# Loading the values of batch 0 once, in slots of three pools, under a newly written order of all steps

## The chip, the cores and the metric

One core of a Trainium2 chip runs the kernel as one program. The time is that of the device in microseconds (us), the median of several executions. The engines are TensorE (PE, with its weight loads as PEld), VectorE (DVE), ScalarE (ACT), GpSimd (POOL) and SyncE (SP), whose queue issues every transfer of this kernel.

## What is computed

A sparse attention and two feed-forward blocks follow one another (4 batches, 8 heads, 576 tokens, 64 numbers a head):

```python
scores = scale * np.matmul(q, k.transpose(0, 1, 3, 2))
thresh = np.max(scores, axis=-1, keepdims=True) - tau
scores = np.where(scores >= thresh, scores, -1000000000.0)
attn = softmax(scores)                                # exp, divided by its sum
x = np.matmul(attn, v)                                # 2304 tokens x 512
h = x @ w_in                                          # 2304 x 2048
g = P(h) / (Q(h) + 1e-06)                             # cubic over quadratic
x = g @ w_out                                         # 2304 x 512
y = ((x @ w1) * (x @ w2)) @ w3 @ w_out2               # 2304 x 512
```

## The kernel before

Every product that feeds the second decimal half of the result is made of two half-precision parts, a high one and a low one ("split"), so that most matmuls come in threes. The heads are taken in pairs: four pairs `c` for each batch `b`. A pair is worked through in two units: `u=0` takes the query blocks 0 and 1, `u=1` the blocks 2, 3 and the short block 4.

One block goes through these steps: `qk` (scores on PE, two PSUM tiles "S"), `top` (row maxima on DVE), `thr`, `exp` (on ACT, its second half on ACT or DVE), `recip`, `p_norm`, `p_hi` and `p_lo` (split of the probabilities), and `p_t` (a transposing DMA into a tile "pT"). When all blocks of a unit are there, `pv` multiplies by the values on PE and `x_split` takes the result from PSUM.

The values of a pair are raw `f32` numbers in DRAM. Their scale is found per batch: `square_v` (ACT) sums the squares of five of the nine row groups of each pair, and `scale_v` makes the power of two. `split_v` then makes the tiles "vh" and "vl" of a pair, in two instructions. In the kernel before, `load_v` brings the values twice: five row groups (320 KB) for `square_v`, and later all nine (576 KB) for `split_v`. Both go into one of the three slots of the pool "wr", which the raw weights (`raw_w`, 512 KB each) use as well. The pool "pT" has three slots too.

The weights are loaded raw, put together again by `conv_w` (two instructions), squared (`square_w`) and, for `w_in`, reduced over PE (`norm_w`) to a scale (`scale_w`). Only with that scale can `split_w` make the two parts of any piece of `w_in`, and only then can the first `h_product` start. `w_product` folds `w3` and the last weight into one matrix ahead of that. After it come `h_product`, the activations, `turn` (a transposing DMA) and `y_product` for each token tile of the first block, and `ab_product`, `turn` and `o_product` for the second.

The order of all these steps is written out by hand as a text, `ORDER`. A token such as `54v.0.1` is event 54, its engine ("v" or nothing DVE, "a" ACT, "p" POOL), and the slots of the tiles that it opens. An event with several parts stands there several times. Each engine, and SP's queue, runs its instructions in the order of the text, so that a transfer whose slot is not yet free holds back all transfers that stand behind it.

Of the kernel before, what the change touches and what calls it, by code (L numbers as in the profile page):

```python
# [16 lines left out]
AF = mybir.ActivationFunctionType  # L17
# [15 lines left out]
0 49.0 4.1 51p.0 5.0.0 51.0 15.0.1 1 16v 53.2 55v.1 55.1 6.1 7.1 26.0.1 29.0 28.0 30 22.2.3 32p.0  # L33
31p.0 31.2 34.0.4 36.5 36a 34a 13.2 24a 38a 38 40v 54.0.1 56.1 42a.6 44p 8.1 58 9.0 3 10.0 11.1
159.7.8 21.1 12 48p.0 12.0 50 46.0 18.0 60v.1 62.1.1 62a 52.1 12 14v.0.0 14 23a.1 17.2 20v.1.1
23.3 64.4 64a 94.0.1 66p 66 68a 20 19a.0 37.0 96.2 76p.5 98 78 90.0.6 100v.2 39p.1 25.1 70a.4 80
39.4 27p.1 72v 74 19.5 102.2.1 104.5 102v 41.2 27.6 57.1 104v 106p 123.1.0 106 117v.4 119 109a
125.3 111p.2 113v 92a 45.0 33.1 115.2 127 43a.0 43.7 63.2 82.0.0 47a.1 47.8 86.0 161v 129a.0 121.0
131.3.3 133.5 131a 57 65v.0 35p.1 35.9 133a 163.0.1 57 165.0 167 169v.1 84a 171.4.1 171a 65.10
173.2 135p 88v.2.2 135 77.1 173a 79p.1 145a.4 88 118.2 79.11 137a 191.0.1 84 81.0 67.1 147 149  # L40
193.1 195 120p.0 120.12 57 71.0 71 198p.2 200.5.0 59a.13 83v.1 139p.6 83.14 202.5 69p.0 200a 202a
228.0.1 204a 204 105.2 175a 175 185v.4 107a.1 177a 108.0 141p 143 214a.3 69.15 110a.0 71 122.1
230.2 187 216 232 110.16 189.1 234a.0 236.6.5 238.2 124v.0 124.17 238a 236a 85.1 85 71 73a.18
256.0.1 95.0 151.0 179p.6 181v 258.3 153a 107.19 645.1 153 260 647v.0 262a.1 218 91.2 112.0
224.4.7 264.7.8 266.1 266a 85 240v 264a 647.20 97p.1 174.1 240 93p.0 97.21 242a 93.22 206a 250v.3
226v 292 625.0 85 252 294.0.1 295.0 297 126.2 112 183.0 112 208p.2 87v.23 176a.1 112 254.2 299v.2
176.24 114v.25 617.1 301.0.6 302.3 116.0 268p 268 128v.0 270v 128.26 210p 628p.1 272v.0 628.27
651.1 212 301a 134.0 302a 654v.1 654.28 274p 278a.2 99.0 166.2 304p 304 168a.0 2 155.1 617 136p.1
617 244v.8 617 280 136.29 306v 246v 130.1 282 168.30 313v.1 157v.3.3 157 315 318.1.0 320.1 150.0
308p.7 620a.31 152v.1 99 152.32 322 323p.0 138.0 325.1.5 142.2 144a.0 288.2.3 144.33 656.1 656 656  # L50
99 309p 99 631.1 327.6 327v 634p.1 325v 634.34 329p 182.0 213.2 343.1 101a.35 329 637.0 215a.0 637
637 158.1 184p.1 637 656 184.36 215.37 221.0 190.2 330a 332v.4 160a.1 345.2 160.38 223v.0 659a.39
223.40 132.1 140 639v.41 146.1 623.0 154.0 220.0 148 290a 346v.1 197.1 199p.1 222a 334v 348.2.5
192v.0 192.42 229.0 199.43 205.2 156 222 156 231v.0 231.44 348v 245.1 170.1 162.0 164.0 172 207p.1
207.45 178.0 180 186.1 188 188 350a 371.0.1 89.0 373.3 194.0 196.1 201.1 203 209.0 247p.0 225.1
211 227.0 237.0 248.0 247.46 374 239v.1 233.0 350 352p 239.47 235 217.1 219 219 249.0 331.2 333p.0
# [1177 lines left out]
```

## Time and profile before

| what | value |
|---|---|
| time, median of 3 (lowest to highest) | 1035.44 us (1033.13 to 1037.77) |
| profiled execution: its time, its span | 1034.65 us, 1032.8 us |
| PE busy | 966.9 us, 94% of the span |
| DVE, ACT, POOL busy | 811.3, 662.0, 313.7 us |
| moved by DMA | 154.63 MB, mean 150 GB/s |

A share of the whole span is an average over stages with different limits. So the profile is read by stretch: which engine is busy without gaps there, and what PE, which is the busiest, waits for.

### The profile page before, as it was taken

The numbers are of one execution on the slowest core, as the hardware profiler recorded it, in microseconds if no ns is written. First come the engines' busy times: TensorE is split into PE (matmuls) and PEld (weight loads), VectorE is DVE, ScalarE is ACT, GpSimd is POOL, SyncE is SP. The second block draws the span as 40 slices with busy tenths as digits, with TensorE's granted clock in tenths as the row PEclk, the third lists the DMA queues.
The fourth block names the chain that finished last, engine by engine and source line by source line (L and its number), as shares of the span: only waits on it lengthen the run. The fifth ranks groups of instructions, "written<-read, shape, count | busy, mean of one in ns | idle before, by whom it ended". The sixth has DMA issues, their size and how long they took to land. (4 is left out here: it accounts for less than half of the span.)

```text
span 1032.8 us, 15597 instructions
## 1 busy us (share of the span) xinstructions
PE 966.9 (94%) x5280; PEld 462.6 (45%) x5284; DVE 811.3 (79%) x1595; ACT 662.0 (64%) x1227; POOL 313.7 (30%) x345
## 2 busy tenths in 40 slices
PE   2599887799999999999999999999999999999998
PEld 1244343344444445554444454544544445444443
DVE  4667789998777998889889989889878857676831
ACT  4464589987657798788647787787664434454510
POOL 2223233424322324233332432333423121223210
PEclk9999989899999999999999999999999999999999
DMA  7999797777757785899665768776666444444332
GB/s 240 243 251 260 250 238 207 185 201 175 189 113 151 157 174 103 172 197 178 126 134 104 143 131 177 153 149 134 129 123 119 93 90 88 80 65 71 62 72 61
DMA packets 334623, 154.63 MB, mean 150 GB/s; under 512 B 307408, under 2 KB 311504, under 8 KB 334544
## 3 DMA queue, kind: packets, MB, share of 16 engines
q1 hardware_dynamic: 334544, 153.65, 66.6%
q8 instruction: 41, 0.67, 0.3%
q14 instruction: 38, 0.31, 0.1%
HBM read 69.98 MB, written 8.13 MB: 76 GB/s over the span
## 5 line engine op out<-in xcount | busy, mean ns | idle before, releaser
L868 PE MATMUL y<-wp,gt 128*128 128x512 f16 x864 | 200.0, 379 | 0.9 <-DMA gt<-gg 0.8
L804 PE MATMUL h<-wp,xp 128*128 128x512 f16 x768 | 179.7, 382 | 3.5 <-DVE U L826 2.9
L975 PE MATMUL h<-wp,yy 128*128 128x512 f16 x576 | 132.2, 379 | 1.1 <-ACT r L819 0.5
L868 PEld LDWEIGHTS <-gt 128*128 128x128 f16 x864 | 82.8, 98 | 105.2 <-issue 6.5
L521 DVE TENSOR_REDUCE m<-S 128x1 f32<-128x576 f32 x144 | 104.7, 750 | 17.1 <-PE S L512 11.7
L804 PEld LDWEIGHTS <-xp 128*128 128x128 f16 x768 | 73.6, 99 | 99.0 <-issue 14.6
L512 PE MATMUL S<-raw 64*128 64x288 f32 x512 | 87.7, 449 | 20.4 <-ACT p L548 10.3
L1004 PE MATMUL y<-wp,gt 128*128 128x512 f16 x432 | 100.2, 379 | 0.0
L812 ACT ACTIVATE U<-h,cf 128x512 f32<-128x512 f32 x72 | 55.8, 775 | 62.9 <-PE h L804 42.0
L975 PEld LDWEIGHTS <-yy 128*128 128x128 f16 x624 | 60.1, 98 | 76.0 <-issue 6.0
L543 ACT ACTIVATE S<-S,th 128x576 f32<-128x576 f32 x107 | 74.7, 712 | 28.3 <-DVE th L359 15.9
L352 POOL TENSOR_TENSOR gg<-A,r 128x512 f16<-128x512 f32 x38 | 52.2, 1374 | 125.9 <-DVE A L847 74.7
L352 POOL TENSOR_TENSOR hl<-p,hl 128x576 f16<-128x576 f32 x48 | 64.6, 1348 | 70.6 <-DVE hl L340 32.3
L548 ACT ACTIVATE p<-S,xy 128x576 f32<-128x576 f32 x107 | 78.9, 742 | 2.9 <-DVE hl L352 0.5
L512 PEld LDWEIGHTS S<-raw 64*128 64x128 f32 x512 | 48.4, 195 | 60.7 <-ACT p L548 19.2
L834 ACT ACTIVATE r<-A,lnb 128x512 f32<-128x512 f32 x72 | 51.8, 721 | 34.8 <-DVE A L352 19.0
L843 DVE SCALAR_TENSOR_TENSOR gg<-U,cf,r 128x512 f16<-128x512 f32 x72 | 56.3, 783 | 20.9 <-ACT r L836 11.7
L352 POOL TENSOR_TENSOR A<-A,r 128x512 f32<-128x512 f32 x37 | 48.3, 1305 | 78.0 <-ACT r L819 75.0
L925 PE MATMUL h<-cw 128*128 128x512 f32 x128 | 60.8, 629 | 9.8 <-DVE cw L680 8.8
L680 DVE SCALAR_TENSOR_TENSOR cw<-rw,head 128x512 int32<-128x512 int32 x72 | 51.9, 725 | 18.3 <-POOL head L340 13.7
L1004 PEld LDWEIGHTS <-gt 128*128 128x128 f16 x432 | 41.7, 98 | 51.5 <-issue 2.2
L728 PE MATMUL y<-cw,dg 128*128 128x512 f32 x112 | 61.8, 634 | 3.0 <-ACT wp L336 1.6
(196 smaller groups left out, 1676.9 us busy)
## 6 DMA issues: line engine op xcount, KB each, us to landing
rw<-in_moe_w_dram SPq DMA_DIRECT2D x32, 511.8 KB, 4.5
rw<-in_moe_w_out_dram SPq DMA_DIRECT2D x24, 511.8 KB, 4.8
raw<-in_k_dram SPq DMA_DIRECT2D x32, 288.0 KB, 3.4
wr<-in_v_dram SPq DMA_DIRECT2D x16, 576.0 KB, 4.8
rw<-in_moe_w_in_dram SPq DMA_DIRECT2D x16, 511.8 KB, 4.3
wr<-in_v_dram SPq DMA_DIRECT2D x16, 320.0 KB, 3.4
out_dram<-A SPq DMA_DIRECT2D x16, 256.0 KB, 2.4
d_y<-x SPq DMA_DIRECT2D x13, 256.0 KB, 2.4
```

The costliest lines, as they stand in the source:

```text
L352: (nc.gpsimd if eng[0] == "p" else nc.vector).tensor_tensor(o, x, y, op=op)
L512: nc.tensor.matmul(t[s][:, half, :HS], x[r, o:o + 128], y[r, keys], start=True, stop=True)
L521: nc.vector.tensor_reduce(st["m", b, c, blk][:, s:s + 1], t[:, :, :HS], axis=AX.XY, op=ALU.max, negate=True)
L543: nc.scalar.activation(t, t, AF.Prelu, bias=th, alpha=BIG)
L548: nc.scalar.activation(x, t, AF.Exp, bias=xy[:, 0:1], accum_out=su)
L728: nc.tensor.matmul(y, st["dg", dg], r, start=True, stop=False)
L804: nc.tensor.matmul(t, x[:, y, c, o:o + 128], w[:, a, :], start=c + i == 0, stop=c == KD - 1 and i == 2)
L843: stt(p[:, 0, :], u, cf[:, 3:4], r, ALU.add, ALU.mult)
L868: nc.tensor.matmul(st["y", n], x[:, 4 * a + j, :], w[:, y, :], start=f + j + i == 0, stop=f == 3 and j == 3 and i == 2)
L925: nc.tensor.matmul(t, st["cw", ("w3", m, j // 4)][:, o:o + 128], st["cw", ("wo2", j)], start=j == 0, stop=j == 7)
L975: nc.tensor.matmul(t, x[:, 4 * y + c, :], w[:, a, :], start=c + i == 0, stop=c == KD - 1 and i == 2)
L1004: nc.tensor.matmul(st["o", n], x[:, 4 * a + j, :], w[:, y, :], start=hf + j + i == 0, stop=hf == 1 and j == 3 and i == 2)
```

## The change

For batch 0 the five-group load is gone. `load_v` with nine groups is called in its place, ahead of `square_v`, which reads the first five groups of that tile; the tile stays until `split_v`. Pair 0 keeps its place in the pool "wr", pairs 1, 2 and 3 go into the three slots of the pool "pT", which the transposed probabilities use afterwards. Batches 1 to 3 load as before. All steps stand in a new order, and many have another engine.

```diff
 ORDER = """
-0 49.0 4.1 51p.0 5.0.0 51.0 15.0.1 1 16v 53.2 55v.1 55.1 6.1 7.1 26.0.1 29.0 28.0 30 22.2.3 32p.0
...
-2527.1 2527 2533 2533 2449 2521 2534a.1 2534
...
     def load_v(b, c, n):
-        t = T("wr", [128, 9, 2 * D])[:, :n, :]
+        t = T("wr" if b or c == 0 else "pT", [128, 9, 2 * D])[:, :n, :]
...
-        nc.scalar.activation(j, st.pop(("vr", b, c, 5)), AF.Square,
+        nc.scalar.activation(j, st.pop(("vr", b, c, 5)) if b else st["vr", b, c, 9][:, 0:5], AF.Square,
...
-            at(load_v, b, c, 9)
+            if b:
+                at(load_v, b, c, 9)
             at(split_v, b, c)
...
     def norms_v(b):
         for c in range(NP):
-            at(load_v, b, c, 5)
+            at(load_v, b, c, 5 if b else 9)
```

The text of the order has 3958 tokens before and 3954 after. Written out, the places of some steps (counted in tokens) are these:

| step | before | after |
|---|---|---|
| first `load_v` of pairs 0, 1, 2, 3 of batch 0 | 2, 12, 35, 39 | 29, 28, 36, 19 |
| second `load_v` of the same pairs | 26, 48, 111, 282 | none |
| last part of `split_v` of the same pairs | 55, 66, 140, 297 | 57, 67, 50, 232 |
| `pv` of the first unit of the same pairs | 108, 203, 359, 428 | 127, 194, 346, 430 |
| last `raw_w` of `w_in` | 404 | 380 |
| first matmul of `split_w` of `w_in` | 442 | 451 |

And these are the engines that the letters name:

| step | before: DVE, ACT, POOL | after: DVE, ACT, POOL |
|---|---|---|
| `exp`, second half | 37, 107, 0 | 30, 114, 0 |
| `conv_w`, first half | 22, 18, 32 | 29, 19, 24 |
| `p_hi`, first head of a pair | 23, 26, 31 | 16, 28, 36 |
| `p_lo`, first head of a pair | 32, 0, 48 | 26, 0, 54 |
| `den` | 35, 0, 37 | 31, 0, 41 |
| `split_v`, first half | 8, 8, 0 | 5, 11, 0 |
| `scale_q` | 11, 16, 5 | 6, 16, 10 |

## Rows read from the trace of the kernel before

**Rows 1.** The page: busy time of the engines, share of the span, instructions.

```profile
PE 966.9 (94%) x5280; PEld 462.6 (45%) x5284; DVE 811.3 (79%) x1595; ACT 662.0 (64%) x1227; POOL 313.7 (30%) x345
```

**Rows 2.** Busy time by stretch; behind it granted clock, DMA share, GB/s.

```profile
0.00:47.00 47.00, 18.43 (x74) 9.35 (x76) 24.95 (x56) 22.80 (x47) 11.93 (x22) 1.00 0.84 239
47.00:120.00 73.00, 68.23 (x229) 31.24 (x226) 50.78 (x91) 34.14 (x65) 20.23 (x27) 0.95 0.92 257
120.00:135.00 15.00, 8.82 (x53) 4.62 (x50) 12.17 (x26) 12.96 (x26) 6.94 (x7) 0.82 0.91 259
135.00:208.00 73.00, 58.66 (x266) 25.52 (x262) 66.11 (x142) 67.42 (x140) 26.94 (x28) 0.90 0.80 206
208.00:316.00 108.00, 104.98 (x540) 49.15 (x542) 88.48 (x204) 75.36 (x142) 31.23 (x33) 1.00 0.70 170
316.00:988.00 672.00, 667.94 (x3952) 324.81 (x3951) 558.39 (x1059) 443.83 (x801) 211.78 (x224) 1.00 0.63 126
988.00:1033.00 45.00, 39.87 (x185) 17.92 (x183) 10.39 (x20) 5.44 (x9) 4.69 (x5) 0.97 0.29 65
```

**Rows 3.** Waits of PE up to 210 us: in total, times, longest.

```profile
PE S L512 <- ACT p L548: 9.6, 4, 4.9
PE h L925 <- DVE cw L680: 8.8, 3, 6.6
PE h L696 <- ACT sq L687: 3.7, 5, 2.0
```

**Rows 4.** Waits of SP's queue up to 135 us: in total, times, longest.

```profile
SPq L669 <- DVE cw L680: 27.4, 21, 4.0
SPq L584 <- DVE cw L680: 13.9, 4, 6.0
```

**Rows 5.** The timeline around the first split of the input weights.

```profile
118.64 5.32 SPq L669 DMA_DIRECT2D rw<-in_moe_w_in_dram  x3
...
125.31 4.50 ACT L687 ACTIVATE sq<-cw 128x512 bf16<-128x512 f32 x8
...
135.47 1.52 PE L728 MATMUL y<-cw,dg 128*128 128x512 f32 x2
```

**Rows 6.** DMA issues: count, KB each, median us from issue to landing.

```profile
wr<-in_v_dram SPq DMA_DIRECT2D x16, 576.0 KB, 4.8
...
rw<-in_moe_w_in_dram SPq DMA_DIRECT2D x16, 511.8 KB, 4.3
wr<-in_v_dram SPq DMA_DIRECT2D x16, 320.0 KB, 3.4
```

**Rows 7.** Groups by line, shapes kept apart: busy us, mean ns of one.

```profile
L352 POOL TENSOR_TENSOR hl<-p,hl 128x576 f16<-128x576 f32 x48 | 64.6, 1348 | 70.6 <-DVE hl L340 32.3 <-ACT hl L336 31.0 <-DVE sc L439 2.9
...
L546 DVE SCALAR_TENSOR_TENSOR p<-S,th,p 128x576 f32<-128x576 f32 x37 | 29.7, 812 | 8.6 <-ACT p L541 7.8 <-issue 0.9
...
L352 DVE TENSOR_TENSOR hl<-p,hl 128x576 f16<-128x576 f32 x32 | 24.8, 776 | 3.2 <-ACT hl L336 1.9 <-POOL hl L340 0.8
```

**Rows 8.** One DVE line with two inputs in SBUF: min/median/max ns.

```profile
L845 DVE SCALAR_TENSOR_TENSOR A<-A,gg x72: 672/691/1648, 162.1 to 979.2; 128x512 f32<-128x512 f32 x72
```

More of the change, by code (lines that the diff above doesn't have):

```diff
@@ new lines @@
+93.2 207 110 248 112a.25 652.1 621.1 211 256 258v.1 260.7.2 95a.1 136.1 650.26 95.27 262.3 652
+237v 124.0 260a 262a 126v.0 624p.1 264v 219.0.5 97 264 221a 266a 624.28 274v.8 276 97 99a.29
+290.1.0 126.30 291.0 87.0 163.2 293 165v.1 613.0 148.1 165.31 150v.0 652 140.0 150.32 213 627.2
+295p.2 297.0.4 298.3 298a 613 142p.1 142.33 240p.6 297a 314.0.1 316.1 318 319v.0 630p.0 73.0 210.1
+288 321.1.5 630.34 212v.1 212.35 613 321a 613 616a.36 619.0 250.0 218.0 300p 339.0 300 302v 242p
+341.2 278 179.2 181v.0 633.0 128.0 155.1 220p.1 304p.1 309p.7 220.37 311 157p.1 633 633 284.0.8
@@ new lines @@
+157.38 633 305v 635a.39 181.40 268a.3 652 655v.41 187.0 215.0 217v 217 189p.1 194.1 226.2 342a.1
+189.42 270v 130.1 234.0 196v.0 344.2.4 196.43 202.1 344v 236p.1 286a 365 138 159.0 658.1 161.0
+167.0 169 175.1 183.0 228v.0 228.44 323.2 177 185 185 151.1 241.2 144.0 146 153 323a 325p 191.0
+193.0 367.0.1 153 312.1 236.45 244.2 204v.0 222.1 224.1 243p.1 198.0 325 346p 204.46 326v 369.3
+370 372p.2 200 206.1 208 327.0 214.0 216 243.47 216 328p.7 330v 230.1 232 238.0 239 272 333v.6
+245.1 247 247 638.0 114.1 346 335 329p.0 249 280.0 249 277v.48 438.0 283a.49 257a.50 279v.51
@@ new lines @@
+482 357a.1 487 479a.0 392p.0 409 345.0 660 357.34 482 490p.1 660.0 660 491.7.1 361.0 392.2 493.2
+491a 414 493a 487 527.1 474p.7 394.0 359.0 364v.1 664p.1 481 439.1 495p 364.10 366.0 489.0 509.1
+511.0 283.1 310.0 689.2 722.0 489 281a 396 495 396.0 396 399v.0 527 283a 424v.26 489 512p.0
+672a.37 691a.0 691.23 417v.32 476p 455.3.8 456p 529.1 529.0 514.0.5 529.1 514a 489v 477.1 496.0
+497a 496 403v.33 773.2 417.0 417a 401v.30 413a.22 531 531 725a.1 401.1 401a 681v.31 499.0 498v.4
+500p 440.1.1 540.0.1 539 674v.40 413.0 534p 776v.0 430.7 403.1 542.2 544 501 403v 473.1 406v.38
@@ new lines @@
+431a.46 432.1 499.1 413a 408v.44 776.42 504a.6 433v 677v.35 433 502 546p.2 431.1 420a.43 672.0
+725.45 422v.47 700.1 431a 672a 434v.5 435.1 711.2 427v.9 434.1 492.2 505 536 499.0 516a 424.0
+547.1.1 442.0 516 549.7 503p 536 434a 703v.0 501 545.0 703.16 549a 547a 551p 518v 408.1 545
+436a.24 538.1 415v.7 424v 714a.1 506 427.0 538 686a.21 538 408a 538p 565.1.0 714.18 483.0 506
+449.1 551 427a 519p.4 422.1 437a 415.0 507 451.0 446.2 761.1 410v.34 437 422v 410.1 444.0 694.0
+415a 560a.2 567.1 569 698.1 706.0 410v 562 508.0 508 521v 406.0 708 570p.1 572.2.0 572a 406a 457.1
@@ new lines @@
+716v 719a 719 1193.1 721v 1193 695.1 927p.23 927.1 927a 702p 786.1.0 789.3 791 644p 1198a.1 676a.4
+678p 794v.2 1196.0 646.0 1196 796.7.5 779 925v.20 799.1 680 796a 1201 799a 1201p.0 1151.1 925.0
+1151 1201p 933v.42 738.0.1 1204.2 615a.1.1 933.1 933a 741.0 743 746p.1 615 925a 1154.0 1154
+1157v.1 747.0.4 614.1 747a 750.6 724p.7 726p 608 1159 1170.0 1170 729.2 1159p.1 1159p 1176 750a
+752a 730v.3 1162.0 800a 800 697a.3.3 820.0.1 822.2 1176a.0 733 752 755a 813v.7 1209.0 1176v 1209
+816 1215a.1 614 757p.0 760p 1212.0 825 697 1212 618.0 623 764a.2 767 618.0 1179.1 1165.1 782.8.1
@@ new lines @@
+727 810.1 705 1080.0 907.5.6 909.7 909a 907a 912p 912 736 736 937 780.0 784 810 861a 645 941.0.1
+784 914a 881v 740.0 811.1 844 740 740 705p 710.1 780.0 679 780.0 679 788v 792 740p 744.0 814.1
+814.1 814.1 939 943.0 944 946p.0 853.0 883v.3 885p 792 895.2 715 887.0 715 819 819 845.1 845
+947.3.0 917a.2 797.1 949.5 823v 828 797 797 797p 802.2 856a 856 924a.4 926 949a 947a 950p 929 950
+918p 921 850.0 952a 854 854 749 749 828 831.0 754.2.1 754 963.1.0 964.2 966 953p.3 936.7.6 955p
+850.0 850.0 858p 880.0 957.1 758a 968v.2 880 969.4.8 758 762.0 831 831 831v 771 836.1 931.1 806.1
@@ new lines @@
+1060 1050 1061a 1020.1 1020 1116.3 1117 1105a.8 1419 1106p 1119a.2 1121.5.0 1121v 1043.0 1020
+1020p 1052 1423 1122.3 1122v 1043 981 1063a.4 932 1432.3 1045.0 928 1136.0 1064p 1124v 1088.1.2
+1124 1045.1 1004 1138.0 1131v.5 1125v 1423p.0 1133 1089v 1139a.1 1078.0 1437.1 1163 1437 1423v
+1113.1 1141.3.7 1141a 1142a 1142 1144v 1023.1 1066.3 1164.1.0 1135 1045.0 1051v 1441a.1 1166.2
+1167 1054 1048 1048 1054 1169a.0 1171.4.6 1004 1026 1026 1146p.4 1056.1 1056 1425.2 1071.1 1056
+1056v 1171a 1435 1172.5 1172a 1067.0 1069v 1186.1.0 1174a 1069 1081.0 1086 1174 1029.0.0 1175v
@@ new lines @@
+1216a 1079 1206 1087 1090.0 1237.0 1079v 1200p 1239 1202 1453.0 1448.1 1453 1082.2 1090.0 1090.0
+1230 1093 1093 1241p.0 1243.1.7 1243v 1217a.4 1244.5 1244v 1448 1095p 1219p 1246p 1220.0 1457
+1232.1.8 1246 1040 1062 1248a 1250a.2 1251p 1253.2 1260.0.1 1457v.1 1225.1 1291v.3.3 1255v.3 1291
+1457v 1262.2 1156.1 1234a 1222.0 1264 1266v.2 1224v 1084 1224 1227a 1098 1098 1257 1084 1101.0
+1101 1109.0 1101 1267.7.6 1269.4 1269a 1267a 1101v 1104.0 1271a 1109 1271 1280a.0 1273v 1227
+1296.1.0 1298.1 1112.1 1112.1 1275p.7 1247.1 1299 1247 1727.2 1282 1112.1 1158a.2.2 1249.0 1622.2
@@ new lines @@
+1358.0 1132 1746 1331p 1242.1 1464a.0 1134v 1316.1 1316.0 1744.1 1320p 1322 1322 1285.0.0 1134
+1245.0 1137.1 1245 1360 1730 1143 1319.0 1325.1 1762.3 1331 1333v 1325 1751a.0 1354v 1362p.2
+1363.3.6 1340v.7 1342 1344 1365.3 1325 1287v 1284.1 1325p 1287 1363a 1365a 1627.1 1140 1367p
+1335a.1 1284 1337v 1744 1367 1369a 1286.1 1376v.4 1381.1.0 1383.2 1748.0 1385 1286.1 1288 1386a.1
+1748 1286.1 1339 1263 1388.4.0 1753 1753a.0 1753p 1755.1 1390.8 1388a 1390a 1346.0 1347a 1378 1288
+1379.2 1290p 1293 1392p 1392 1401v.7 1347 1402 1293 1404 1295.0 1295 1295 1295p 1767.1 1767
@@ new lines @@
+1771v.0 1917.2 1413.1.0 1415.1 1394a 1417 1265.0 1395a.1 1265 1268.1 1263 1418a.0 1268.1 1268.0
+1420.6.3 1422.8 1422a 1270 1327.2 1270 1297.0 1757 1769.1 1757 1272p 1332.0 1332 1769 1370v.4 1274
+1372v 1274 1277.1 1277 1277 1464 1277v 1279.1 1760a.0 1420a 1397p 1424v 1329.1 1334.1 1334.1
+1334.1 1438.0.1 1774 1329 1350.1 1424 1426v 1433v.7 1440.3 1774a.0 1442 1350 1774v 1760 1427a.0
+1281 1429v 1281 1300 1466.6.2 1468a 1434 1352.0 1352.0 1352.0 1336 1443p.2 1445.0.5 1374.0 1431.1
+1410.3.8 1776.2 1336 1781.0 1447.4 1300 1781 1355 1445v 1447v 1338p 1341 1341 1449v 1449 1343.1
@@ new lines @@
+1608a 1564v 1577.1 1561 1668.1.0 1662a.7 1669.3 1664 1566 1577.0 1566 1993.2 1522 1655a 1671
+1568.0 1982.1 1982 1996 1609a.2 1657v.8 1659v 1592 1673a.0 1582v 1393 1675.1.0 1568 1676.3 1676a
+1568 1538.1 1618.1 1620v 2000.3 1639p 1660.1 1584 1796.0 1692.0 1694.0 1696a.2 1996 1580 1541
+1611v 1568p 1584 1587.1 1541 1620 1587 1587 1587p 1698.0.5 1698a 1675a 1634.0 1571.0 1543.0.0
+1699a 1543 1594.0 1594 1699 1545v 1701a 1613.8 1615.1 1703a.4 1545 1724.0.1 1550 1722 1678p 1616a
+1616 1678 1636 1636.1 1687v.2 1636 1689 1596.1 1573.0 1596.0 1596.1 1612.1 1666.0 1573 1680a 1612
@@ new lines @@
+1759 1780 1661.1 1661 1998a.0 1998 1782v 2023v.0 1663.1 1663.1 1663.1 1667p 1552 1745 1768a.0 1610
+1803.0.1 1805.0 1761a 1807 1770 1665 1809v.1 1763a.5 1765p 1628 1628 1631.1.0 1631 1670 1784p.3
+1811.3.6 1633a 1670 1712.0 1766 1665 1747.0 1633 1635.1 1672.1 2016.1 1812.4 1713a 1717a.3.3
+1642.1 1642 1812a 1672 1713 1672 2021.0 1644.1 2021 2016 1644.0 1644.0 1717 1649v 1786p 1811a
+1788.1 1814p 2025 1772 1800.5.8 1672v 1647 1814 1647 2025a.0 1651 1651 1828.1.0 1789.0 1830.2 1832
+2025p 1793.1 1802a 1791v 1640 1823a.3 1791 2028.1 1679.0 1825 1679 1795v 1834v.2 1816a 1818p.0
@@ new lines @@
+1896.0.4 1707 1880p 1860.5.8 1882.2 1896a 1862a 1709.1 2239 1898.6 1898a 2242a.0 1709 1709 1810.0
+1899p 1833.0 1833 1899 1901a 1709p 1711.1 2245 2507 1908a.7 1910 1924.1.0 1903v.6 1836.1 1836.1
+1815.1 1926.0 1928 1836.0 1905p 1907 1885 2032a.0 1887.0 1930p.2 1931.1.4 1933.0 1695 2245p.0
+1931a 1815 1838 1838 1852.0 1852 1840v 1842 1842 1933a 1935p 2032 2245v 1949.1.0 1845.1 1845
+1813.1 1845 1817.0 1845p 1854.1 1854.0 1820 1695 1912 1951.2 1953 1921.6.1 1854.1 1954a.0 1714
+1714 1820 1956.5.5 1958.8 1958a 1856 2036p 1813 1956a 1847.2 1856 2255.0 1922p 1716.3.1 1981.0.1
@@ new lines @@
+1817.1 1935 1817.0 1822p 2253.1 2253 1937v 1938v.7 1940v 1942.1 1716 1718v 2247.1 1718 1983.1
+2250.0 1985 1986v.1 1824 1824 1721.0 1826.0 1826 1725 1826 1826p 1988.2.4 2255 1829.0 1990.7
+2258a.0 1881.1 1858v 1861 1861 2261 1960a 1863.1 1988a 1990a 1914.0 2234 1863 1915a 2006.0.1 1960
+1944a.1 1992v 2250 1863 1962a 2008.3 1915 2010 1963a.6 2261a.0 1946 1947.0 1965p 2011v.2 2013.7.0
+2261p 2013a 1967 1969a.5 1970 1863p 1881 2263.1 1884.1 1900.0 1831 1884.1 1900 1884.0 1972 1723
+1992 2015.1 1902.0 2015a 1902.0 1831 1849 1849 2266 1886 2266 1902.1 1886 1978.8.6 1974.1 1906v
@@ new lines @@
+1879 2269v.1 2288.0 2298v.1 2047v 2033a 2049a 1929.1 2087p.2 1929 2296.0 2296 2033 2059.1 2059
+2049 1929 2057a.8 2290.0 2080 2088.0.0 2088a 1916 2062.0 2090a 2301 1929v 2062.0 2090 2064 2301p.0
+2064 2038.0 2301p 2038 2050v 2062.0 2067v 2070 2040.1 2070 1932.1 2072.1 2072 2058 2072 2506.2
+2269 2040.1 2072p 2290 2109.0.1 2040.1 2383.0 1936.1 2046v 2304.0 2076p 2043 2048 1936 2052a.1
+2043 2111.3 2053p 2108 1939.0 2112 1939.0 2114p.0 1939.0 1943p 2048 1941 2306 1916 1945 2306
+2115.4.4 2051.0 1941 2075.2 2051 2051 1945 2117.7 2117a 2060.1 2051v 2386.0 2082 1948.1 2386 1934
@@ new lines @@
+2385.1 1948 1948 1948v 1950.0 2115a 2119p 2055.0 2385 2119 2387a.1 2388 2388v.1 2104.8.6 2131.1.0
+2133.0 2081.1 2135 2081 2077 2083.0 2083.1 2388v 2102.0 2136v.1 2092p 2083.1 2089p 1934 1952
+2138.1.3 2054.1 1952 2309v.0 2086 2138a 2139.1 2086 2154.1 2155.2 1955.0.0 2384 2139a 2141a 1955
+1957a 2101.1.1 2309 2127v.5 2102 2103a 2128 1957 1959.1 2103 2120v 2105.1 2106p 2056.0 2391.1
+2389.0 2141 2105.0 2122p.2 2391 2056 2105.0 2130.2 2123v 1964 2157v.2 2158.5.7 2107 2107 2078
+2158a 2093v.4 2125.0 2392.0 2110v 2392 1961 2178 2091 2091 2095p 2398.3 2094.0 2094 2149a.5 2096.0
@@ new lines @@
+2078 2179.0.1 2094 2094v 2393a.0 2406.1 2394 2406 2097.1 2181.1 2182 2113 2113 2184a.0 2186.2.2
+2186a 2151 2152 2116.1 2187.4 2160a 2116 2187a 2116 2116v 2400.0 2400 2118.2 2201.0.1 2402a.1
+2098.0 2100a 2160 2100 2099 2203.3 2205 2401.0 2394a.0 2206a.1 2401 2099 2208.7.1 2162v 2163a.5
+2394p 2209.6 2403 2208a 2209a 2514.0 2189p 2189 2197v.0 2198 2190v 2224.1 2225.0 2227v.2 2165v
+2166.4 2229.3.8 2229v 2211p 2403v.1 2143v 2514 2403v 2192v.7 2193p 2395.1 2230v 2515 2211 2213p
+2219a.2 2230 2121 2232v 2121 2124.1.0 2508.1 2124 2126v 2126 2134.0 2134 2137.0 2404.2 2508 2195.1
@@ L278 @@
+2495a.0 2484.1 2484 2447 2448.1 2488p 2501v.1 2502 2522.0 2522 2496 2528.1 2528 2529 2523 2496a.1
+2529 2477 2489.0 2502p.0 2523 2382 2502p 2492 2496p 2530v.0 2497.2 2524v.1 2490 2525 2498.0 2503.1
+2498 2525p.1 2504 2490 2525p 2504 2526.2 2531 2531p.0 2505v.0 2531p 2532.0 2491a.1 2491 2505
+2527.1 2527 2533 2533 2449 2521 2534a.1 2534
 """
```

383 lines of the change are left out of this document (139 added, 244 removed).

## The prediction

> **What bounds the kernel now.** I read the page first, then the busy time by stretch, then the waits of PE and of SP's queue in the first fifth of the span, then the timeline around one gate, and last the durations by group and the DMA issues. The page says that PE is busy for 966.9 us of 1032.8 [rows 1]. So at most 66 us can be won without taking work from PE, and the change takes none from it. Where those 66 us lie is what the stretches tell [rows 2]. PE is idle for 28.6 us of the first 47 (47 − 18.43), for 4.8 of the next 73, for 6.2 of the 15 up to 135 us, and for 14.3 of the 73 up to 208. That is 53.9 us. Behind 208 us it is idle for 3.0, 4.1 and 5.1 us, the last of these at the tail. From 208 us on PE sets the pace, and a change there can only do harm or take away some of 12 us. Ahead of 208 us something else sets the pace, and that is where the change works.
>
> It is not the same thing all the way. Up to 135 us the 16 DMA engines are busy for 0.84, 0.92 and 0.91 of the time and move 239 to 259 GB/s, while ACT is busy for 57 us of the first 120 (22.80 + 34.14) [rows 2]. SP's queue waits there mostly for DVE's `cw`, which frees the "wr" slots: 27.4 us for weights and 13.9 us for transposes [rows 4]. Transfers set this pace. The stretch ends at a gate: the last three pieces of `w_in` are issued from 118.64 us on, the last near 122.7, ACT squares eight pieces without a gap for 4.50 us, and the first matmul of `split_w` starts at 135.47 us [rows 5]. From there to 208 us DVE is busy for 66.11 and ACT for 67.42 of 73 us, and the DMA share falls to 0.80 [rows 2]. Those two engines set the pace there. PE's own waits up to 210 us name ACT and DVE and only few microseconds each [rows 3]: they say what came last, and the stretches say why that was late.
>
> **The change, part by part.** *Loads removed.* Four loads of 320 KB go: 4 × 327,680 bytes = 1.31 MB. At the 257 GB/s of the stretch from 47 to 120 us that is 5.1 us. I counted all transfers that stand in the text up to and with the last `raw_w` of `w_in`: 30,656 KB before, 29,376 after. The difference, 1,280 KB, is the removed loads exactly, so the order puts no other transfer ahead of the gate in their place. Four issues on SP's queue go too; their landing, 3.4 us each [rows 6], overlaps other transfers and I count nothing for it. Bounds: 0 if the queue's waits and not the bytes set the pace, 5.1 us if the bytes do. DMA shares above 0.9 are nearer to the second. **−5.1 us** at the gate.
>
> *Slots.* The three tiles in "pT" leave more of the "wr" slots to weights at the beginning, which can only help the queue there; nothing counted. Against it, pair 3 keeps its "pT" slot until token 232, so the transposes of pairs 1 and 2 have two slots and stand behind `pv` of the pair before them. Behind such a transpose on SP's queue stand the next weights, and `conv_w`, `w_product` and the gate wait for these. The row for this kind of wait is transposes behind `cw`, 6.0 us at the longest [rows 4]; what is already in flight when the queue stops covers about one landing, 4.3 us for a weight [rows 6]. So one such wait costs 6.0 − 4.3 = 1.7 us to 6.0 us of transfers, or nothing where PE comes to `pv` in time. By the text, the PE work ahead of `pv` of pairs 1 and 2 is 33.1 and 79.0 us, against 32.5 and 79.5 before. I take 0.
>
> *Engines and order.* I gave each step of both texts the mean duration of its group, kept apart by shape [three of them in rows 7], and added them up along the text. For the whole text the sums change by −22.4 us on DVE, +10.3 on ACT and +26.4 on POOL; PE's is the same. `exp` shows the pattern: seven second halves leave DVE at 812 ns each. `p_lo` shows the other: six go from DVE's 776 ns to POOL's 1348 ns [rows 7]. Such sums overstate, since neighbours overlap at their ends: before, they give 76.6 us on ACT and 73.0 on DVE between the gate and the point where PE has done 136 us of its work, which is the stretch from 135 to 208 us with 67.42 and 66.11 busy [rows 2]. I scale by 0.9.
>
> Up to the gate ACT's sum rises from 74.2 to 81.2 us; ACT has gaps of 63 us in the first 120, which hide these 7.0 us. If that cover is gone the gate is later by up to 7.0 us. From the gate to PE's 136 us, ACT's sum falls from 76.6 to 66.3 us and DVE's from 73.0 to 67.2. But it comes back: to the point where PE has done 166 us (before, at about 237 us) the sums from the gate on are 103.0 before and 102.2 after on ACT, 103.2 and 99.5 on DVE. PE's order behind 208 us waits for whichever engine is later, so of this part I take what ACT leaves, 0.8 × 0.9 = 0.7 us. Bounds: 0, and 0.9 × 10.3 = 9.3 us if nothing of it comes back. **−0.7 us.**
>
> Behind that, PE is the bound and its order is much the same: the same tiles at the same amounts of PE work, within 10 us. The last product is that of the same tile, so the tail stays. I looked for tight places: the PE work that stands between a `turn` or the last `p_t` and the product that needs it. What is missing to one landing (3.1 to 3.4 us) adds up to 80 us over all products before and 84 after, and of the 80 only 7.1 us show as idle time of PE from 208 to 988 us [rows 2]. The change in that is below 1 us; 0 taken.
>
> **The sum.** 1034.65 − 5.1 − 0.7 = 1028.9 us for the profiled execution, which lies 0.8 below the median of the three runs. I predict **1029.0 us**, −0.6%. A measurement of this kernel tells about 0.5%, or 5.2 us, from no change, so this is just beyond that line.
>
> **A rule weighed.** POOL's sum to PE's 166 us rises from 66.8 to 71.8 us, and a DVE line with two SBUF inputs shows what can come of it: its median is 691 ns and its longest 1648 [rows 8]. The Trainium skill, "SBUF — State Buffer", "Who interferes with whom", says that a DVE instruction with two SBUF inputs and a GpSimd instruction that reads SBUF share one port pair, and that the second to start is blocked until the first is done. The long cases of that line agree with it, and its median says that most pass free. If each added microsecond of POOL held DVE for one, the time would be that of the third rival below.
>
> **The rivals.**
> 1. *The queue takes it back* (0.17). One transpose of pairs 1 to 3 blocks SP's queue behind `pv` as priced above, 1.7 to 6.0 us, middle 3.9: 1028.9 + 3.9 = 1032.8, no change. For it: two "pT" slots up to token 232. Against it: PE's work ahead of those `pv` is the same as before.
> 2. *The bytes are not what sets the pace* (0.08). The weights wait for "wr" slots anyhow, and the loads removed were hidden: 1034.65 − 0.7 = 1034.0, no change. For it: 27.4 us of SP's waits for `cw`. Against it: DMA engines busy for 0.92.
> 3. *DVE is held up by POOL* (0.08). DVE's 5.0 us: 1028.9 + 5.0 = 1033.9, no change. Against it: the median of 691 ns.
> 4. *ACT sets the pace from the start* (0.16). Its sum to PE's 166 us is 183.4 after and 177.2 before; if ACT had no gaps, PE would come there 6.2 us later: 1034.65 + 6.2 = 1040.9, slower by 0.6%. It decides if the added 7.0 us of ACT ahead of the gate do not fit into ACT's gaps. For it: between the last load of `w_in` in the text and the first split, ACT has 14.7 us of work against 5.7, and it was busy for 12.96 of 15 us there [rows 2]. Against it: the gaps of 63 us up to 120 us, into which all but the last squares can go, since they need earlier weights.
>
> The forecast itself has 0.51; its own range is 1022 to 1030.
>
> **Chances and range.** Faster by over 0.5%: 0.50, which is the forecast with its better side (the 9.3 us of DVE and ACT kept would give 1034.65 − 5.1 − 9.3 = 1020.3) less a little, since it lies so near the line. Within 0.5%: 0.34, rivals 1 to 3 with 0.33 and that little. Slower: 0.16, rival 4. The range goes from 1020 (all of that better side) to 1041 (rival 4).
>
> **What would show it.** In the profile after: the first matmul of `split_w` near 130 us in place of 135.47; 1.31 MB less moved; PE idle for about 48 us up to 208 in place of 53.9; DVE's busy time down by about 20 us, ACT's up by 9, POOL's up by 25; PE's busy time the same within a few microseconds; idle time behind 208 us still near 12. The prediction is wrong if the gate does not move, or if it moves and PE's idle time reappears behind it: then ACT or DVE, by their busy time between the gate and 237 us, or a transpose in front of `pv`, by PE's waits on L599, would be the place to look.

## The result and the profile after

The changed kernel takes 1027.06 us, median of 5 runs (1023.36 to 1027.6), against 1035.44. The ratio is 0.9906, 95% interval 0.9877 to 0.9934. I had said 1029.0, and faster, so the forecast came out; the terms behind it did not, as the experiments show.

The page after, with the busy time that answers to [rows 1]:

```profile
span 1024.9 us, 15572 instructions
PE 965.1 (94%) x5284; PEld 463.7 (45%) x5284; DVE 798.6 (78%) x1559; ACT 666.7 (65%) x1235; POOL 337.7 (33%) x373
DMA packets 334048, 153.34 MB, mean 150 GB/s; under 512 B 307344, under 2 KB 311440, under 8 KB 333968
```

PE's work is the same, and 1.29 MB less is moved. The stretches after, columns as in [rows 2]:

```profile
0.00:47.00 47.00, 20.79 (x50) 10.30 (x50) 27.69 (x59) 25.68 (x48) 10.33 (x19) 0.93 0.83 254
47.00:120.00 73.00, 68.57 (x264) 32.13 (x265) 52.25 (x99) 39.11 (x77) 21.47 (x29) 0.99 0.88 245
120.00:135.00 15.00, 9.69 (x47) 4.70 (x43) 13.40 (x43) 10.55 (x22) 7.83 (x9) 0.70 1.08 243
135.00:208.00 73.00, 64.73 (x316) 30.11 (x317) 65.83 (x129) 69.49 (x145) 27.27 (x33) 0.93 0.89 216
208.00:316.00 108.00, 107.44 (x568) 50.82 (x567) 89.61 (x198) 78.44 (x142) 44.33 (x44) 1.00 0.71 165
316.00:988.00 672.00, 662.92 (x3907) 321.99 (x3906) 541.25 (x1018) 441.41 (x802) 220.10 (x232) 1.00 0.62 125
988.00:1026.00 38.00, 30.95 (x143) 13.66 (x141) 8.57 (x17) 2.00 (x3) 6.35 (x7) 0.96 0.34 70
```

Against [rows 2], PE is idle up to 208 us for 44.2 us in place of 53.9, and 6.1 us of the 9.7 gained lie in the stretch from 135 to 208. From 208 to 316 it is idle for 0.6 in place of 3.0. From 316 to 988, though, it is idle for 9.1 us in place of 4.1: something is given back there.

The split of `w_in` starts at 131.76 us instead of 135.47 [rows 5]. The waits of PE up to 210 us and of SP's queue up to 135 us, which answer to [rows 3] and [rows 4] (lines behind 660 are one higher now):

```profile
PE S L512 <- ACT raw L338: 15.4, 2, 9.6
...
PE h L697 <- ACT sq L688: 4.6, 8, 1.3
PE S L512 <- ACT p L548: 4.2, 2, 2.7
```

```profile
SPq L670 <- DVE cw L681: 34.9, 24, 4.0
...
SPq L584 <- PE h L599: 3.3, 1, 3.3
```

The queue's waits for a "wr" slot have grown from 27.4 to 34.9 us. All rows of its waits up to 135 us together have fallen, though, from 92.8 to 80.1 us: the queue as a whole waits less.

To see where along the way the time goes, I put the same matmuls of both traces beside each other. The table gives the start of PE's n-th matmul as the trace has it (us), and for each other kernel how much earlier (−) or later it starts that one than the kernel before; the last line is the span. The orders differ a little, so the n-th matmul is not always the same step, but PE's work up to it is nearly the same. Four matmul records are missing from the trace before (5280 against 5284), between 118 and 290 us; behind them the leads of after, f3, f2, f1 and g1 stand up to 0.9 us too high. The kernels e1 to g1 are those of the next section.

```
n        before   after     e1     e2     f3     f2     f1     e4     g1     e8
100        60.0    -3.9   -2.9   -4.2   -3.5   -0.2   -4.0   -4.4   -3.2   -0.8
300       120.4    -7.1   -2.9   -6.0   -6.1   -1.3   -7.3   -5.4   -5.5   -1.2
400       154.2    -6.6   -3.0   -6.3   -1.4   -1.9   -7.0   -6.1   -4.7   -1.4
600       205.1   -11.5   -3.5  -11.5   -2.2   -2.3  -12.3  -11.3   -9.9   -1.6
1000      285.9   -14.3   -3.5  -13.7   -2.1   -1.7  -14.7  -14.2  -12.0    0.0
1400      358.2   -16.2   -3.5  -15.3   -2.3   -3.9   -7.1  -15.8  -13.6    0.1
1800      428.7   -16.2   -3.5  -13.2   -2.6   -2.6   -7.4  -15.0  -13.7    4.9
2600      560.2   -16.4   -3.5  -13.0   -1.9   -2.2   -7.7  -11.2  -13.7    5.9
2800      589.7   -16.5   -3.5  -13.2   -1.1   -2.4   -6.9   -9.9  -11.7    5.9
3400      682.8   -13.6   -2.5   -9.8   -1.9    0.3   -6.5   -6.7  -11.4    8.9
4200      824.6   -10.7   -2.4   -7.1   -1.9    3.5   -6.5   -4.9  -10.5   15.0
5200     1010.4   -10.0   -2.5   -6.6   -2.0    3.8   -6.6   -4.5  -10.6   15.2
span     1032.8  1024.9 1030.6 1027.3 1031.9 1038.4 1028.1 1028.3 1023.0 1048.7
```

So the changed kernel has 7.1 us of its lead at 120 us already, ahead of the gate, makes 9.1 us more by 360 us, and gives 6.5 us back between 590 us and the end (−16.5 to −10.0). My sum had 5.1 us at the gate, 0.7 behind it, and nothing given back.

### The profile page after: what moved, and what is told of

Its sections match the earlier page's. It is cut to its first block, busy times and chain, and to the rows that moved or that the text cites. A ratio compares the mean times of both kernels' runs of the same rounds, so it can differ in the third digit from the quotient of the medians.

```text
span 1024.9 us, 15572 instructions
## 1 busy us (share of the span) xinstructions
PE 965.1 (94%) x5284; PEld 463.7 (45%) x5284; DVE 798.6 (78%) x1559; ACT 666.7 (65%) x1235; POOL 337.7 (33%) x373
## 4 chain that ended last, share of the span: by engine, by line
PE 66%; DVE 14%; ACT 9%; DMA 5%; issue 3%; POOL 1%; SPq 0%; DVEq 0%; ACTq 0%; POOLq 0%
PE y L869 13%; PE h L805 12%; PE h L976 9%; PE y L1005 6%; PE S L976 6%; PE S L512 6%; PE h L926 5%; PE h L599 3%; PE y L729 3%; DVE m L521 2%; ACT p L548 2%; DMA gt<-gg 2%; ACT S L543 2%; DMA pT<-hl 1%; PE S L507 1%
## 5 line engine op out<-in xcount | busy, mean ns | idle before, releaser
L543 ACT ACTIVATE S<-S,th 128x576 f32<-128x576 f32 x114 | 78.9, 710 | 25.0 <-DVE th L359 14.8
L352 POOL TENSOR_TENSOR A<-A,r 128x512 f32<-128x512 f32 x41 | 54.0, 1316 | 112.8 <-ACT r L820 111.1
L352 POOL TENSOR_TENSOR hl<-p,hl 128x576 f16<-128x576 f32 x54 | 72.8, 1350 | 49.5 <-ACT hl L336 23.8
L548 ACT ACTIVATE p<-S,xy 128x576 f32<-128x576 f32 x114 | 84.1, 742 | 3.0 <-DVE hl L349 1.1
L813 ACT ACTIVATE U<-h,cf 128x512 f32<-128x512 f32 x72 | 55.8, 776 | 36.2 <-DVE A L848 18.5
L835 ACT ACTIVATE r<-A,lnb 128x512 f32<-128x512 f32 x72 | 51.7, 718 | 34.1 <-DVE A L352 18.2
L825 DVE SCALAR_TENSOR_TENSOR U<-h,cf,U 128x512 f32<-128x512 f32 x72 | 53.6, 745 | 24.9 <-ACT r L820 10.2
```

Of the source, the lines that this page charges most:

```text
L352: (nc.gpsimd if eng[0] == "p" else nc.vector).tensor_tensor(o, x, y, op=op)
L543: nc.scalar.activation(t, t, AF.Prelu, bias=th, alpha=BIG)
L548: nc.scalar.activation(x, t, AF.Exp, bias=xy[:, 0:1], accum_out=su)
L813: nc.scalar.activation(u, h, AF.Identity, bias=cf[:, 15:16], scale=cf[:, 0:1])
```

## The experiments

**Are the loads worth 5.1 us?** Two kernels: the loads taken out of the old order, and put back into the new one.

```diff
     def load_v(b, c, n):
+        if b == 0 and n == 5:
+            places.clear()
+            return
...
+        ones = unit.to_broadcast([128, 640])
-        nc.scalar.activation(j, st.pop(("vr", b, c, 5)), AF.Square,
+        nc.scalar.activation(j, st.pop(("vr", b, c, 5)) if b else ones, AF.Square,
```

> The order of before, with the four 320 KB loads of batch 0 for the squares left out and nothing else moved (the squares of batch 0 are taken of a constant, so the scale of batch 0 is another number and the output of batch 0 with it). Theory 1, the bytes: 1,280 KB less ahead of the gate at 257 GB/s are 5.1 us, measured in the changed kernel 3.7 us at the first split_w matmul (135.47 to 131.76), and they pass to the end: 1030 to 1032 us, first split_w matmul at 130 to 132. Theory 2, the order gives the gain and the queue takes the bytes back: 1034 to 1036 us, first split_w matmul at 134 to 136.

```diff
+    def again(c):
+        t = sb.tile([128, 640], F32, name="again", tag="xp1", bufs=1)
+        nc.sync.dma_start(out=t, in_=v[0, c, :, :640])
+    AGAIN = {("wo2", 0): 0, ("w3", 2, 0): 1, ("in", 0, 0): 2, ("in", 2, 0): 3}
     def raw_w(key, src, i):
+        if key in AGAIN:
+            again(AGAIN[key])
```

> The changed kernel with four loads of 320 KB more ahead of the gate, into a tile that nobody reads. Theory 1, the bytes: the gate goes back by 4 to 5 us and the end with it, 1030 to 1032 us. Theory 2, the order gives the gain: 1026.5 to 1028 us, since the lead is made between the gate and PE's 200 us of work.

Without the loads the old order takes 1033.88 us, ratio 0.9986 (0.9976 to 0.9997) to the kernel before: 1.5 us, with 0.3 to 2.5 in the interval. The table shows a lead of about 3 us from the first hundred matmuls on, with 2.5 left at the end. The last piece of `w_in` is issued at 120.80 us in place of 123.62 (I had read 122.7 there), and the gate opens at 132.25 us in place of 135.47. The issue before, then the issue and the first matmul of `split_w` without the loads:

```profile
123.62 0.33 SPq L669 DMA_DIRECT2D rw<-in_moe_w_in_dram  x1
```

```profile
120.80 0.33 SPq L675 DMA_DIRECT2D rw<-in_moe_w_in_dram  x1
132.25 1.12 PE L734 MATMUL y<-cw,dg 128*128 128x512 f32 x2
```

So the time lies just under theory 2's range, but the gate lies next to theory 1's 130 to 132. The new order with the loads takes 1028.72 us, ratio 0.9933 (0.9915 to 0.9951), between the ranges of both theories; against 0.9906 that is 2.8 us more, with an uncertainty of 3.4, so that alone settles nothing. Its split of `w_in` starts at 131.44 us, no later than the 131.76 of the changed kernel, and its lead at n = 1000 is 13.7 us against 14.3. What it loses it loses behind n = 1400, where no load was added. (The tile of the added loads shares the slot `xp1` with a tile of the kernel, which can cost a wait of its own.)

So in the old order the loads are worth about 3 of the 5.1 us at the gate, and at the gate of the new order nothing that shows. And most of the lead that the changed kernel has ahead of the gate is not theirs: with the loads put back it is 6.0 us at n = 300, against 7.1. Its order, engines and slots make that part together. A possible reason for the small worth of the loads stands in the waits of SP's queue up to 135 us, of the old order without the loads and of the new one with them:

```profile
SPq L675 <- DVE cw L686: 32.0, 23, 3.9
```

```profile
SPq L678 <- DVE cw L689: 38.9, 27, 4.0
```

In the old order, 5.1 us of transfers go and the queue's waits for a "wr" slot rise from 27.4 [rows 4] to 32.0, by 4.6 us. But all rows of the queue's waits together are 90.2 us in place of 92.8. In the new order, four loads come back and the waits for a slot rise too, from 34.9 to 38.9, with three more of them; from 47 to 120 us the engines then move 256 GB/s in place of 245. And `f1`, which has the text of the changed kernel up to there, shows 37.6 in this row. So that the slots took back what the bytes gave is not shown.

A caution on the gate: single profiles scatter there. Kernels with one and the same text ahead of it show the split at 131.76, 131.56 and 133.61 us (after, f1, g1), and at 135.47 and 133.94 (before, f2). The 3.7 us between the two profiles that I compared are not much more than that scatter, and against `f2` the gate of `e1` is only 1.7 us earlier.

**Where is the lead made?** The new order up to a point, and behind it all steps that are left in the order of before. `e3` changes over at the gate and `e7` at about 265 us; both give out the slots of all tiles anew, by the one that came free first in the text.

```diff
 ORDER = """
 ... 376a 251p.0 277.0
-277a 438 438 438 282v ...
+348p 285.2 271a.1 282v 259.1 ...
```

> The changed kernel's order up to the first split_w, then the order of before for all that is left; the single loads stay. Theory 1, the bytes: the gate's 3.7 us alone, 1031 to 1032 us. Theory 2, the lead of 11 to 14 us is made by the order behind the gate: the lead at PE's 200 us of work is then about 4 us instead of 14.3. If the end loses nothing without the new tail, both give about 1031 us; if the order ahead of the gate already carries the lead, 1021 to 1024 us.

```diff
 ... 877.42 855 879.0
-663p.1 526 602v 855 903.0 ...
+937 699.1.2 526 588 579v.5 ...
```

> The changed kernel's order up to about 265 us (PE's 197 us of work), then the order of before. The lead there is 14 us in the changed kernel. Theory A, the tail of the new order is what gives 6 to 7 us back: 1020 to 1022 us. Theory B, a lead is eaten whatever the tail: 1026 to 1028 us.

They take 1043.24 us (ratio 1.0078, 1.0061 to 1.0094) and 1046.45 (1.0098, 1.0084 to 1.0113): slower than either kernel, which no theory had. The same splice at 552 us, `e4`, takes 1032.08 (0.9964, 0.9948 to 0.998), and the opposite one, `e8`, 1050.59 (1.0139, 1.0123 to 1.0156): these two, too, lie in no theory's range.

```diff
 ... 1521.0 1373 1377 1459
-1408v 1506.1 1506 ...
+1968 1486v.1 1436.0 ...
```

> The changed kernel's order up to about 560 us, then the order of before. Theory A, the new order's own tail is tighter and costs 6 to 7 us: the lead of 14 to 15 us is kept, 1020 to 1022 us. Theory B, any lead is eaten behind 560 us since the other engines did not gain as much as PE: 1026 to 1028 us, like the changed kernel.

```diff
 ... 1497 1507.2.3 1507a
-1381 1480v 1381 ...
+1410.1 1480p 1377 ...
```

> The order of before up to about 575 us, with its four loads, then the changed kernel's order. Theory A, the new tail itself costs 6 to 7 us: 1040 to 1042 us. Theory B, what is given back is the lead being eaten, and without a lead nothing is: 1034 to 1036 us.

`e8` tells why. Up to n = 2600 it has the steps, engines and loads of before, and still it loses 4.9 us between n = 1400 and 1800 and is 5.9 behind at 2600. Only slots differ there, in 450 tokens. The waits of ACT and of PE around 400 us in `e8`:

```profile
ACT hl L336 <- DMA pT<-hl: 3.7, 1, 3.7
```

```profile
PE h L975 <- DVE U L342: 3.1, 1, 3.1
```

ACT wants to write an `hl` whose slot a transposing DMA still reads. The kernel before has neither wait in that stretch. So these four kernels don't tell the order from the slots, and I made them again with another rule: each tile takes the slot of the tile that it follows in its own kernel. Only a few steps are on the wrong side at the chosen places, and the slots ahead of a splice are those of the kernel itself.

```diff
 ... 198.0 325 346p
-204.46 326v 369.3 370 ...
+114.1 326a 328v.7 330v ...
```

> The changed kernel's order up to 121 us, then the order of before, slots by the same rule. Theory G, the order behind the gate makes most of the lead: the lead is 4 to 5 us at 121 us and stays 2 to 4 us, 1031 to 1034 us. Theory H, the order and the loads ahead of the gate make it: a lead of 11 to 14 us by 290 us, 1022 to 1026 us.

This one takes 1035.23 us, ratio 0.9993 (0.9983 to 1.0003): no gain at all, and just outside theory G's 1031 to 1034. Its lead is 6.1 us at n = 300, and 1.1 to 2.6 from n = 400 on, where the changed kernel goes on to 16. But it loses those 4.7 us right at the seam. Its waits of DVE from 110 to 140 us and of PE from 100 to 155 us hold these:

```profile
DVE hl L340 <- DMA pT<-hl: 2.8, 1, 2.8
```

```profile
PE h L697 <- ACT sq L688: 8.3, 8, 3.7
```

DVE waits once for an `hl` slot that a transposing DMA still reads. A `cw` comes behind that, then ACT's square of it, and PE waits 3.7 us for the square; the gate opens at 134.45 us. Neither the kernel before nor the changed one has that wait of DVE there, and PE waits for the squares for 3.7 and 4.6 us in them. So the own slots did not keep this seam clean, and `f3` does not tell theory G from theory H: whether the lead made ahead of the gate would last without the seam stays open.

What the changed order adds behind the gate can be read from the kernels that go on in it. From n = 400 to n = 1000 the lead grows by 7.7 us in the changed kernel, 7.7 in `f1`, 7.3 in `g1`, 8.1 in `e4` and 7.4 in `e2`. `e4` has other slots in that stretch, so the growth does not hang on one choice of them.

**Engines or order?** Each order with the other's engine letters; 633 letters change, and slots are given anew (654 and 770 tokens).

```diff
-... 30v.0 ... 15a ... 54a.1 ... 31v ... 33v ...
+... 30p.0 ... 15v ... 54v.1 ... 31a ... 33a ...
```

> The changed kernel's order and loads with the engines of before for every step. Theory L, the choice of engines makes the lead between the gate and PE's 200 us of work (about 7 to 10 us): 1033 to 1037 us. Theory O, the order of the steps makes it: 1026 to 1029 us.

```diff
-... 16v ... 55v.1 ... 31p.0 ... 36a ... 34a ...
+... 16a ... 55a.1 ... 31v.0 ... 36v ... 34v ...
```

> The order and the loads of before with the engines of the changed kernel for every step. Theory L, the choice of engines makes the lead: 1026 to 1030 us. Theory O, the order makes it: 1034 to 1038 us.

1136.01 us (1.0957, 1.0939 to 1.0976) and 1146.75 (1.1072, 1.1053 to 1.1091): both theories fell, by 100 us. `e8`, with new slots and the new tail together, lost 15 us, so most of this is likely the letters, though no run separates them from the slots. ACT in the first and DVE in the second wait for their partners more than in the kernel with the same order (there 18.2 and 18.5 us for ACT, 11.7 and 5.5 for DVE):

```profile
ACT th L357 <- DVE m L521: 38.9, 14, 11.9
ACT U L813 <- DVE A L848: 31.7, 12, 5.3
```

```profile
DVE gg L843 <- ACT r L836: 24.1, 20, 4.2
DVE su L563 <- ACT su L357: 19.7, 11, 4.4
```

An order and its letters are one plan. What the letters alone would be worth in this change can't be told.

**Why is part of the lead given back?** Splices at 318 us, slots by the second rule: new then old, and old then new.

```diff
 ... 684 873a 834
-837v 1184v.0 662v 1184 ...
+1080.2 1074.0 1075.0.0 1221.1 ...
```

> The changed kernel's order up to its 318 us, then the order of before, and each tile of the tail takes the slot of the tile that it follows in the kernel before (the spliced kernels until now gave out slots anew). At the splice the lead is 14 to 16 us. Theory A, the new order behind 550 us has its own tight places, which cost 6 us: the lead is kept, 1019 to 1022 us. Theory B, a lead is eaten there in either order: 1026 to 1028 us.

```diff
 ... 877.1.6 879.4 879a
-838v 877a 882p 661 ...
+838v 821.1 661 661 ...
```

> The order of before up to the same step, with its four loads, then the changed kernel's order, slots by the same rule. Theory A, the new order's tail itself costs 6 us: 1040 to 1043 us. Theory B, only a lead is eaten, and here is none: 1034 to 1037 us.

The first takes 1030.79 us (0.9965, 0.9951 to 0.9979), which neither theory gave; the second 1043.34 (1.0074, 1.006 to 1.0088), at the upper end of theory A's range. The table tells them apart. `f1` loses 7 us at the seam, where PE waits 4.2 us for DVE's `U` once. From there on, with the old tail, its lead stays at 6.5 to 7.7 us up to n = 5200: nothing eats it. `f2` has 2.4 us at n = 2800, and with the new tail it goes to +3.8, a loss of 6.2, where the changed kernel loses 6.5. So it is not that a lead is eaten: the new text behind 590 us, order, engines and slots together, is tighter by itself. PE's waits from 600 to 820 us of the changed kernel, then of `f2`, then of `f1`:

```profile
PE h L976 <- DVE xp L349: 1.6, 1, 1.6
PE h L805 <- DVE xl L349: 0.9, 1, 0.9
PE S L507 <- issue: 0.9, 1, 0.9
PE h L805 <- ACT r L820: 0.9, 1, 0.9
PE h L805 <- ACT U L338: 0.8, 1, 0.8
```

```profile
PE h L975 <- DVE xp L349: 1.7, 1, 1.7
PE h L804 <- DVE xl L349: 0.9, 1, 0.9
PE h L804 <- ACT r L819: 0.9, 1, 0.9
PE S L507 <- issue: 0.9, 1, 0.9
PE h L804 <- ACT U L338: 0.7, 1, 0.7
```

```profile
PE y L869 <- DMA gt<-gg: 1.2, 1, 1.2
PE h L599 <- DVE U L827: 0.7, 1, 0.7
PE h L976 <- DVE xp L349: 0.3, 1, 0.3
```

The same five waits, to a tenth and 5.1 us in sum, stand in both kernels with the new tail, with a lead of 14 us and with none, and not in the old tail.

**The new head with the old tail, and the price of slots.** The last kernel has the steps and engines of `e4` and differs in the slots of 711 tokens.

```diff
 ... 1459 1968
-1486v.1 1436.0 1478 ...
+1486v.3 1436.2 1478 ...
```

> The same order, step by step, and the same engines as the kernel spliced at 552 us before (changed up to there, then before), but every tile in the slot of the tile that it follows in its own kernel: 711 steps have another slot and nothing else differs. The lead at the splice is 16 us in the changed kernel. Theory A, the new tail's own tight places cost 6 us and the old tail keeps a lead as it is: 1019 to 1022 us, 5 to 8 us under the changed kernel. Theory A with a seam as at 318 us, where 7 us went in one wait: 1025 to 1028 us. Theory S, slots cost nothing: as the splice before, 1030 to 1033 us.

It takes 1024.73 us (1021.62 to 1024.91), ratio 0.9889 (0.9868 to 0.991), between the two ranges of theory A and below theory S. Against `e4` that is 0.9889 / 0.9964 = 0.9925, or 7.8 us with an uncertainty of 2.7, for slots alone. In `e4` ACT again waits for a transposing DMA, around 490 us; in `g1` it does not:

```profile
ACT p L548 <- DMA pT<-hl: 3.4, 1, 3.4
```

That wait can be only a part of the 7.8 us: by the table `e4` loses 3.8 us between n = 1800 and 2600 and 6.7 us behind that, where `g1` loses none and 3.1. The 6.7 us were not traced to single waits.

Of its lead `g1` gives back 3.1 us from n = 2600 on, 2.0 of them at the seam, where the changed kernel gives back 6.4. It ends at 10.6 us of lead, less than theory A's plain case, since this profile had only 13.7 at the splice. By its median it is 2.3 us below the changed kernel, but the two ratios are 0.17% apart with an uncertainty of 0.35: that it is the faster one is not shown.

## Why the prediction came out, step by step

**Loads, −5.1 us.** Part of the mechanism was there and the size was off: taking out the loads gave 1.5 us by time and about 3 in the profile of the old order, and putting them back did not move the gate of the new one. I took the bytes to be what sets the pace, because the DMA engines were busy for 0.92 of the time, and gave the rival that says otherwise 0.08. That share does not say that bytes limit the gate, and the 27.4 us of the queue's waits for `cw` [rows 4] spoke against it. Neither my term nor rival 2 holds in full. That the lead near the gate came out close to my term (3.7 us at the gate's own start, 6.6 at n = 400) is luck: with the loads put back it is 6.3 at n = 400. Most of it belongs to the order, engines and slots ahead of the gate, for which my sum had nothing.

**Slots, 0.** The feared wait behind `pv` is there once, 3.3 us on SP's queue, and nothing shows what it cost. The step that failed is wider: I looked at "wr" and "pT" alone, while the change renumbers the slots of nearly all tiles. That slots alone can be worth 7.8 us is shown by `e4` and `g1`; what the change's own renumbering is worth was not measured.

**Engines and order, −0.7 us.** This is the step that failed most. Behind the gate, from n = 400 to n = 1000, the lead grows from 6.6 to 14.3 us: 7.7 us, near my bound of 9.3 and far from 0.7. I had taken 10.3 us less ACT work up to PE's 136 us and then written "but it comes back". ACT's part does come back, and the lead stays. The 29 us behind the stretch from 135 to 208 us, of before, then both stretches of after, 5 us earlier:

```profile
208.00:237.00 29.00, 28.55 (x136) 13.84 (x137) 27.25 (x55) 24.50 (x48) 6.35 (x7) 1.00 0.76 194
```

```profile
130.00:203.00 73.00, 64.17 (x322) 30.40 (x319) 66.36 (x142) 69.81 (x144) 29.32 (x35) 0.91 0.92 223
203.00:232.00 29.00, 28.44 (x117) 12.80 (x116) 26.05 (x51) 24.83 (x46) 10.52 (x12) 1.00 0.73 190
```

In the first 73 us PE is busy for 64.17 in place of 58.66 [rows 2], 5.5 us more, while ACT is busy for 69.81 in place of 67.42. In the next 29 PE already has 28.5 in both, and ACT only 24.5 and 24.8. The same can be counted from each gate to the same amount of PE's work, of before and then of after:

```profile
135.47:208.00 72.53, 58.19 (x262) 25.43 (x260) 65.83 (x141) 66.95 (x139) 26.54 (x27) 0.90 0.80 206
135.47:237.00 101.53, 86.74 (x397) 39.27 (x397) 93.08 (x195) 91.45 (x186) 32.88 (x34) 0.93 0.79 203
```

```profile
131.76:199.00 67.24, 58.63 (x290) 27.20 (x289) 60.70 (x129) 64.05 (x133) 27.29 (x32) 0.92 0.91 223
131.76:227.00 95.24, 86.16 (x401) 39.70 (x399) 86.00 (x175) 90.48 (x183) 37.94 (x44) 0.94 0.85 214
```

For some 58 us of PE the changed kernel needs 5.3 us less, with 2.9 us less of ACT and 5.1 less of DVE. For some 86 us ACT's difference has shrunk to 1.0, and DVE's has grown to 7.1. So work put off from a stretch that ACT and DVE limit into one that PE limits seems to cost nothing here. My own rows said that PE sets the pace from 208 us on, and the tally should have stopped there. That the put-off work of ACT makes this lead fits these rows, but so does DVE's lighter load, which does not come back; no run moved either alone, and the cause stays open between them.

**Behind that, 0.** It was +6.4 us, from n = 2600 to n = 5200. I called PE's order there much the same and priced the tight places at landings of DMAs, of which the sum hardly changed (80 to 84 us). The five waits above, 5.1 us in sum, are mostly for DVE and ACT, which I had not counted, since those engines have room on the average.

**The sum.** In the profiled pair, by the table: a lead of 6.6 us up to n = 400, 9.8 more up to n = 2600, 6.4 given back to n = 5200, and 2.1 in the last matmuls (up to 0.9 of that are the missing records), −7.9 of span against my −5.8. My terms were off by −1.5, −9.1, +6.4 and +2.1 us, which leaves −2.1: it came out near because the misses offset, and that is luck.

**Signs named.** First matmul of `split_w`: 131.76 us (near 130 said). PE idle up to 208 us: 44.2 (48 said). DVE −12.7 (−20 said), ACT +4.7 (9), POOL +24.0 (25). PE's idle time behind 208 us is about 16, not 12, and that was the sign that something is lost there.

**The other rivals.** Rival 4: up to 135 us ACT is busy for 75.3 us in place of 69.9, and the gate is not later; the gaps took it. Rival 3: POOL has 24 us more, and the line of [rows 8] reads

```profile
L846 DVE SCALAR_TENSOR_TENSOR A<-A,gg x72: 672/692/1568, 154.4 to 973.7; 128x512 f32<-128x512 f32 x72
```

with a median of 692 ns in place of 691 and a longest one of 1568 in place of 1648; three of the 72 take over 900 ns, and seven did before. The rule of the Trainium skill, "SBUF — State Buffer", "Who interferes with whom", on DVE and GpSimd blocking each other can hold for its few long cases, but here more work on POOL did not lengthen the line.

## What to carry to other kernels

A busy share of the DMA engines near 0.9 is no proof that bytes limit a stage: here 5.1 us of transfers gave 1.5. Look at what the issuing queue waits for, at all its rows and not at one alone. When work is moved along an order, add it up stage by stage, and stop where another engine takes over the pace: past that point it seemed free here, and brought into such a stage it can still cost, at single products that wait for it. An order, its engines and its slots are one plan; splices are worth trying only where the two plans have done nearly the same steps, and with their own slots. Even then a seam can cost as much as what it is to measure: look for its waits first.

## What was not expected of the hardware

Which slot a tile gets, at the same number of slots, the same order and the same engines, moved the time by 7.8 us (uncertainty 2.7). The waits that go with it are of an engine's write for a transposing DMA that still reads the slot's last content: 3.4 us in `e4`, 3.7 in `e8` and 2.8 in `f3`, at places where the kernels with other slots show none. How much of the 7.8 us these waits make was not measured.
